# Two layers of windowed attention and a SiLU feed-forward net: chunk 2 of the first layer also by seven block products for eight

## The chip, the cores and the metric

The kernel runs on one core of a Trainium2 chip. The core has five engines with instruction streams of their own: TensorE (PE, matrix products into PSUM), VectorE (DVE), ScalarE (ACT), GpSimd (POOL) and SyncE (SP). In this kernel POOL and SP mostly issue DMA transfers. Measured is the time of one execution on the device in microseconds (us); lower is better.

## The reference

```python
x = A_x                                             # 1 x 2048 x 576, float32
x = x + _A_ref(_layernorm(x), A_wqkv, A_wo)
x = x + _B_ref(_layernorm(x), B_w1, B_w2)
x = x + _A_ref(_layernorm(x), A_wqkv, A_wo)         # the same weights again
x = x + _B_ref(_layernorm(x), B_w1, B_w2)

def _A_ref(x, wqkv, wo):                            # 32 heads of 18
    q, k, v = split(x @ wqkv)
    idx = pos[:, None] - (arange(8) * 2)[None, :]   # keys at 0, 2, .. 14 positions back
    logits = where(idx >= 0, einsum("bhsd,bhswd->bhsw", q, k[idx]) * 18 ** -0.5, -1e9)
    return einsum("bhsw,bhswd->bhsd", softmax(logits), v[idx]) @ wo

def _B_ref(x, w1, w2):                              # 576 -> 4608 -> 576
    return silu(x @ w1) @ w2
```

## The kernel before, in words

**Precision.** Each float32 operand of a product is split into two float16 parts (high and low), and three of the four partial products are made. A first FFN product over the 576 inputs thus takes 14 matmuls per 128 hidden units (the short last block of 64 inputs is packed), each over 512 tokens: 36 x 14 = 504 a chunk. The second FFN product takes three matmuls per pair of blocks.

**Tiling.** The 2048 tokens are four chunks of 512, so the two layers make eight steps, s = 0 to 7; "chunk 2" below is step 2, the third chunk of the first layer. Each step has a `front` (layer norm, q/k/v, attention in four units of eight heads, projection onto x, and the normalized and transposed input of the FFN), then an FFN. Attention itself runs on DVE: products with the window's keys (L756), sums over a head (L760), a softmax, products with the values (L789), sums over the window (L796, L797). For the first layer q, k and v of all chunks are made in step 0 (`qkv_ahead`) and wait in DRAM (`kd`, `qd`).

**Two FFN forms.** `ffn` is the plain one: a first product z (L1167), SiLU and high part on ACT, low part on DVE (L1174), and the second product in four groups into two accumulators `acc` (L1186), which DVE adds to x (L835). In step 0 it also loads the raw weights, scales and splits them (`raw_load`, `raw_split`), and stores the split forms to DRAM (`w1s`, `w2s`). `ffn_pairs` handles two blocks of 128 hidden units, two halves of the inputs and two halves of the tokens as a 2 x 2 block product, and makes seven block products (`P1` to `P7`) for eight, of 7 matmuls of 256 columns each: 18 x 7 x 7 = 882 a chunk (L1071). Their sums are put together on ACT (L1075) and DVE (L1078), the low part of h is L1104, and the second product is L1125. It needs seven linear forms of the inputs (`forms`, into tiles `xf`) and seven of the weights of each pair. `prepare` makes those of pair q, for q = 0 to 17: it loads raw blocks of w1 (POOL, L966 and L969), takes four sums on DVE (L977), splits them on ACT (L985) and DVE (L992), and stores seven blocks to `wfs[q]`. Before the change steps 0 to 2 use `ffn` and steps 3 to 7 use `ffn_pairs` (the constant S2).

**What sets the order.** The program is laid down by a planner (`Plan`). Each piece of work is given an engine, an assumed duration, what it reads and writes, buffers, and a priority (low first), and is taken when its inputs are there and a buffer is free; the result is one fixed order per engine. Step s has priority s - 1.0 for its front, s - 0.5 for its FFN's work on the other engines, and s + 0.5 for the FFN on PE. `prepare` has a priority of its own, PREP. Tiles of different names share memory as parts of one area (XA, XB, O, WQA, W1A, HSA, YO); the planner keeps two that overlap from being live at once.

## Time and profile before

| | |
|---|---|
| median of 3 runs | 2184.23 us (2181.3 to 2188.39) |
| profiled execution | 2180.11 us, span 2178.3 us |
| PE busy | 2125.9 us, 98% |
| DVE busy | 1585.8 us, 73% |
| ACT busy | 932.0 us, 43% |
| POOL busy | 379.4 us, 17% |
| granted PE clock, mean | 0.998 |

The sum of the prediction is made against the profiled execution, 2180.11 us, which lies 4.1 us under the median of the runs. A row of a group reads: source line, engine, operation, output <- inputs, shape, count, then busy time, mean duration of one in ns, and the idle time of the engine just before, with what ended it. The FFNs of the first layer begin and end on PE at about 227, 460, 699 and 932 us.

### The profile page before, as it was taken

The page shows a single profiled execution, that of the slowest core. Times are in us where ns is not written, and L with a number is a line of the kernel's source. Part 1 is how long each engine was busy: PE and PEld are TensorE (multiplying, and loading weights), DVE is VectorE, ACT ScalarE, POOL GpSimd, SP SyncE. Part 2 cuts the span into 40 slices and gives each one's busy share as a digit, 9 for nine tenths or more (in the row PEclk, how much of TensorE's full clock was granted, in tenths as well). Part 3 has the DMA queues.
Part 4 walks back from the last instruction along what each step waited for, and adds up shares of the span by engine and source line. Part 5 has one row for each costly group of instructions (what it writes and reads, how often), then busy time and mean ns, then how long its engine had stood idle before and what let it go on. Part 6 is the DMA issues. An engine that isn't in the chain of part 4 may idle for free.

```text
span 2178.3 us, 40221 instructions
## 1 busy us (share of the span) xinstructions
PE 2125.9 (98%) x15820; PEld 1540.8 (71%) x15820; DVE 1585.8 (73%) x2479; ACT 932.0 (43%) x1715; POOL 379.4 (17%) x639
## 2 busy tenths in 40 slices
PE   5999999999999999999999999999999999999999
PEld 3555556656766666677788778887688867888887
DVE  7898999999999754457975599646995569852222
ACT  7545677744244334343324434243442424333232
POOL 2124365332234331301100010000000000000000
PEclk9999999999999999999999999999999999999999
DMA  5577577586677675786649675496655855575443
GB/s 160 161 199 271 177 237 237 182 297 218 170 256 255 171 214 167 209 261 192 191 108 246 169 209 174 112 260 158 202 170 141 240 160 149 161 185 174 142 149 108
DMA packets 314006, 416.07 MB, mean 191 GB/s; under 512 B 136904, under 2 KB 237876, under 8 KB 307544
## 3 DMA queue, kind: packets, MB, share of 16 engines
q1 hardware_dynamic: 274832, 279.13, 45.2%
q0 software_dynamic: 35712, 129.17, 18.3%
q10 hardware_dynamic: 3272, 5.19, 0.8%
q8 instruction: 124, 2.03, 0.4%
q14 instruction: 66, 0.54, 0.1%
HBM read 298.47 MB, written 67.68 MB: 168 GB/s over the span
## 4 chain that ended last, share of the span: by engine, by line
PE 71%; DVE 15%; DMA 7%; issue 3%; POOL 1%; ACT 1%; ACTq 0%; SPq 0%; DVEq 0%; POOLq 0%
PE acc L1125 23%; PE z L1071 10%; PE misc L1071 10%; PE acc L1186 7%; PE z L1167 6%; PE z L658 6%; PE misc L658 5%; PE acc L828 4%; DVE pr L789 2%; DVE lg L760 2%; DMA w<-wfs 2%; DVE pr L796 2%; DVE pr L756 2%; DMA wq<-in_B_w_dram 1%; DVE xa L992 1%
## 5 line engine op out<-in xcount | busy, mean ns | idle before, releaser
L1125 PE MATMUL acc<-w,h 128*128 128x288 f16 x4320 | 544.9, 286 | 1.5 <-DVE h L1104 0.7
L1125 PEld LDWEIGHTS <-h 128*128 128x128 f16 x4320 | 422.5, 98 | 108.6 <-DVE h L1104 1.0
L1071 PEld LDWEIGHTS <-w 128*128 128x128 f16 x4410 | 430.8, 98 | 64.4 <-DMA w<-wfs 7.4
L1167 PE MATMUL z<-xb,w 128*128 128x512 f16 x1512 | 331.8, 379 | 6.4 <-ACT w L902 2.0
L1186 PE MATMUL acc<-w,h 128*128 128x288 f16 x2592 | 321.9, 286 | 0.0
L1186 PEld LDWEIGHTS <-h 128*128 128x128 f16 x2592 | 253.7, 98 | 65.7
L1071 PE MATMUL z<-xb,w 128*128 128x256 f16 x2240 | 281.9, 273 | 2.5 <-DMA w<-wfs 1.3
L1071 PE MATMUL misc<-xb,w 128*128 128x256 f16 x2170 | 273.4, 273 | 5.5 <-DMA w<-wfs 4.5
L1167 PEld LDWEIGHTS <-w 128*128 128x128 f16 x1512 | 147.5, 98 | 182.3 <-DVE w L904 3.7
L835 DVE SCALAR_TENSOR_TENSOR x<-acc,d,x 128x576 f32<-128x576 f32 x135 | 109.5, 812 | 192.3 <-PE acc L1125 151.5
L658 PEld LDWEIGHTS <-xa 128*128 128x128 f16 x1344 | 132.3, 99 | 119.6 <-issue 10.1
L756 DVE TENSOR_TENSOR pr<-qt,kv 128x2304 f32<-128x2304 f32 x64 | 163.5, 2554 | 33.6 <-DMA kv<-kv 32.2
L789 DVE TENSOR_TENSOR pr<-kv,pe 128x1152 f32<-128x1152 f32 x128 | 169.7, 1352 | 1.1
L760 DVE TENSOR_REDUCE lg<-pr 128x128 f32<-128x2304 f32 x64 | 163.1, 2548 | 1.2
L796 DVE TENSOR_TENSOR pr<-pr 128x1152 f32<-128x1152 f32 (+1 forms) x128 | 135.2, 1056 | 3.4
L1169 ACT ACTIVATE hs<-z,d 128x512 f32<-128x512 f32 x108 | 73.8, 683 | 123.1 <-PE z L1167 121.4
L1104 DVE SCALAR_TENSOR_TENSOR h<-wq,sh,h 128x1024 f16<-128x1024 f32 x59 | 75.5, 1280 | 60.9 <-ACT h L1101 60.9
L658 PE MATMUL z<-wq,xa 128*128 128x432 f16 x602 | 116.3, 349 | 3.4 <-ACT w L671 3.1
L828 PE MATMUL acc<-wo,yo 128*128 128x288 f16 x896 | 115.7, 288 | 3.3 <-DMA yo<-yh 3.3
L658 PE MATMUL misc<-wq,xa 128*128 128x432 f16 x574 | 111.8, 351 | 4.0 <-ACT xa L448 2.5
L1174 DVE SCALAR_TENSOR_TENSOR h<-hs,sh,h 128x512 f16<-128x512 f32 x108 | 79.6, 746 | 45.6 <-ACT h L1171 45.5
L1075 ACT ACTIVATE wq<-misc 128x256 f32<-128x256 f32 x85 | 32.0, 376 | 187.0 <-PE misc L1071 187.0
(196 smaller groups left out, 2355.1 us busy)
## 6 DMA issues: line engine op xcount, KB each, us to landing
w<-wfs SPq DMA_DIRECT2D x630, 160.0 KB, 3.3
w<-w2s SPq DMA_DIRECT2D x252, 288.0 KB, 4.8
w<-w1s SPq DMA_DIRECT2D x72, 320.0 KB, 4.8
wfs<-xa POOLq DMA_DIRECT2D x18, 1120.0 KB, 5.7
wq<-wqs SPq DMA_DIRECT2D x17, 1080.0 KB, 7.0
kv<-kd POOLq DMA_DIRECT2D x8, 1584.0 KB, 8.2
w1s<-w POOLq DMA_DIRECT2D x36, 320.0 KB, 3.8
w<-in_B_w_dram POOLq DMA_DIRECT2D x36, 288.0 KB, 4.6
```

Of the source, the lines that this page charges most:

```text
L658: nc.tensor.matmul(T(m)[:, :3 * UC], a, b, start=n == 0, stop=n == len(pl) - 1)
L756: nc.vector.tensor_tensor(T(pr), T(qt)[:, j:j + 2, None, :].to_broadcast([P, 2, W, UC]), win(T(kv), j, 2), op=ALU.mult)
L760: nc.vector.tensor_reduce(T(lg)[:, j:j + 2].rearrange("p a w h -> p (a w h)"), T(pr).rearrange("p a w (h d) -> p (a w h) d", d=DH), axis=A ...
L789: nc.vector.tensor_tensor(T(pr)[:, a].rearrange("p w (h d) -> p w h d", d=DH), v, T(pe)[:, j + a, :, :, None].to_broadcast([P, W, UH, DH]) ...
L796: nc.vector.tensor_tensor(t[:, :, 0:h, :], t[:, :, 0:h, :], t[:, :, h:2 * h, :], op=ALU.add)
L828: nc.tensor.matmul(T(acc)[:, h, 0:288], a, b[:, h * 288:(h + 1) * 288], start=n == 0, stop=n == len(pl) - 1)
L835: nc.vector.scalar_tensor_tensor(t, T(acc)[:, :, 0:288], d, t, op0=ALU.mult, op1=ALU.add)
L1071: nc.tensor.matmul(t, w[:, u, :], v[:, r, :], start=first and m == 0, stop=m == 6, skip_group_check=True)
L1125: nc.tensor.matmul(T(acc)[:, h, 0:288], T(hb[t])[:, a, f, j * P:(j + 1) * P], T(wbs[t][f])[:, w, h * 288:(h + 1) * 288], start=t == 0 and ...
L1167: nc.tensor.matmul(T(z), v, u, start=m == 0, stop=m == len(pl) - 1)
L1174: op("DVE", 0.68, lambda hs=hs, h=h, f=f: nc.vector.scalar_tensor_tensor(T(h)[:, 1, :], T(hs), shs[i][:, f:f + 1], T(h)[:, 0, :], op0=ALU. ...
L1186: nc.tensor.matmul(T(acc)[:, h, 0:288], T(hb[q])[:, a, j * P:(j + 1) * P], T(wbs[q][0])[:, w, h * 288:(h + 1) * 288], start=q == 0 and m = ...
```

## The change

Step 2 takes `ffn_pairs` as well (S2 goes from 3 to 2), so its front ends in `forms`, and `prepare` must be through the pairs before that FFN needs them: PREP goes from 1.6 to 0.9, ahead of step 2's attention. What comes with it:

- `forms` of step 2 keeps its second half of sums in a part of the key/value buffers (`yc`), since XA holds the weight forms being made; step 3's attention fetches its second and later units, and writes its output, only after these forms are done. Its first adds take a set of scratch buffers of their own (`ha`).
- `prepare` loads with eight DMAs instead of twelve, and stores its seven blocks as four and three, each from a tile of its own (`wg`, `wh`).
- In step 0 the raw w2 blocks from block 6 on land in XA (`wu`), and the split w1 blocks from 6 on in WQA (`wv`), once the last of the q/k/v products made ahead is done. Until now both shared the slots of `w1` and `w2`.

```diff
-PREP = 1.6
-S2 = 3
+FAR = 6
+PREP = 0.9
+S2 = 2
...
-    part("wg", XA, 1, [7, 5, P], F16)
+    part("wg", XA, 1, [4, 5, P], F16)
+    part("wh", XA, 1, [3, 5, P], F16, at=4 * KB * 2)
...
+    part("kv", KV, 2, [NI, 2, UC], F32)
+    part("yc", KV, 1, [8, KH], F32, at=KVB, turns=False)
...
+    part("wv", WQA, 6, [10, P], F16)
+    part("wu", XA, 4, [2, D], F16)
...
+    parts("ha", [(HSA, 0), (XB, 14 * KB * 2), (YO, 0)], [4, 2 * P], F32)
...
-                   own + [(qt, j) for j in range(NJ)] + [(kv, "halo"), (kv, "edge")], pr_, nbytes=P * 4 * UC * 26, lanes=2)
+                   own + [(qt, j) for j in range(NJ)] + [(kv, "halo"), (kv, "edge")], pr_, nbytes=P * 4 * UC * 26, lanes=2,
+                   after=formed[-1:] if u else ())
...
-                op("DVE", 2.55, tree, [], [(pr, 0), (pr, 1), (o, j, u), (o, j + 1, u)], pr_)
+                op("DVE", 2.55, tree, [], [(pr, 0), (pr, 1), (o, j, u), (o, j + 1, u)], pr_, after=formed[-1:])
...
-        a, b = raws[f] = Buf("w1"), Buf("w2")
+        far = f >= FAR
+        a, b = raws[f] = Buf("w1"), Buf("wu" if far else "w2")
...
-        wab = [(Buf("w1"), Buf("w2")) for f in fs]
+        far = f0 >= FAR
+        wab = [(Buf("wv" if far else "w1"), Buf("w2")) for f in fs]
...
-            for i in range(4):
-                f, h = divmod(i, 2)
-                c = slice((2 * q + f) * P, (2 * q + f + 1) * P)
-                nc.gpsimd.dma_start(t[:, i, 0:2, :], w1[h * KH:h * KH + 2 * P, c].rearrange("(k p) c -> p k c", p=P))
-            for r in range(4):
-                for h in range(2):
-                    nc.gpsimd.dma_start(t[32 * r:32 * (r + 1), h:4:2, 2, :], w1[
-                        h * KH + 2 * P:(h + 1) * KH, 2 * q * P:(2 * q + 2) * P].rearrange("p (f c) -> p f c", f=2))
-        op("POOL", 7.2, load, ["wsc"], [w], prio, nbytes=P * 12 * P * 4, lanes=8)
+            for h in range(2):
+                for k in range(2):
+                    nc.gpsimd.dma_start(t[:, h:4:2, k, :], w1[h * KH + k * P:h * KH + (k + 1) * P, 2 * q * P:(2 * q + 2) * P].rearrange(
+                        "p (f c) -> p f c", f=2))
+                for f in range(2):
+                    v = w1[h * KH + 2 * P:(h + 1) * KH, (2 * q + f) * P:(2 * q + f + 1) * P]
+                    nc.gpsimd.dma_start(t[:, h + 2 * f, 2, :], bass.AP(tensor=v.tensor, offset=v.offset, ap=[[0, 4], *v.ap]))
+        op("POOL", 4.8, load, ["wsc"], [w], prio, nbytes=P * 12 * P * 4, lanes=8)
...
-                hq, h = Buf("hq"), Buf("hp")
+                hq, h = Buf("hq" if s >= NC - 1 else "ha"), Buf("hp")
...
-        XT[s] = layer_norm(X[s], s - 1.0, "xb", s == 1, s == 0) if s < S2 else forms(X[s], s - 1.0)
+        XT[s] = layer_norm(X[s], s - 1.0, "xb", s == 1, s == 0) if s < S2 else forms(X[s], s - 1.0, "yc" if s == S2 else "yb", [("wfs", NP - 1, 1)] if s == S2 + 1 else [])
```

How the planner's order moves is seen at three places. Lines of the new file lie some 9 to 15 higher: L756 and L760 (attention) are L768 and L772 there, L835 is L847, L977 and L992 (preparation) are L991 and L1006, L1071, L1078, L1104 and L1125 (pairs) are L1086, L1093, L1119 and L1140, L1167, L1174 and L1186 (plain FFN) are L1182, L1189 and L1201, L828 (projection) is L840.

DVE at the end of chunk 0's FFN, from its last add to x (tile x_77) on; first before the change. `pr`, `lg`, `pe` and `o` are attention's tiles, `wq` and `xa` here the weights' sums and their splits.

```order
L835 SCALAR_TENSOR_TENSOR x_77<-acc_105,d_269,x_77 128x576
L789 TENSOR_TENSOR pr_89<-kv_83,pe_88 128x1152 x2
L796 TENSOR_TENSOR pr_89<-pr_89 128x2x576
L796 TENSOR_TENSOR pr_89<-pr_89 128x2x288
L797 TENSOR_TENSOR o<-pr_89 128x2x144
L1174 SCALAR_TENSOR_TENSOR h<-hs,sh_267,h 128x512
L756 TENSOR_TENSOR pr_89<-qt_84,kv_82 128x2304
```

After the change the same add is followed by this.

```order
L847 SCALAR_TENSOR_TENSOR x_77<-acc_105,d_268,x_77 128x576
L1006 SCALAR_TENSOR_TENSOR xa<-wq,accw,xa 128x4x256
L1006 SCALAR_TENSOR_TENSOR xa<-wq,accw,xa 128x4x128
L772 TENSOR_REDUCE lg_85<-pr_88 128x128
L1189 SCALAR_TENSOR_TENSOR h<-hs,sh_266,h 128x512
L1006 SCALAR_TENSOR_TENSOR xa<-wq,accw,xa 128x3x256
L1006 SCALAR_TENSOR_TENSOR xa<-wq,accw,xa 128x3x128
```

The preparation now stands among chunk 2's attention from here on, which moves later by as much.

DVE at the end of chunk 1's FFN, from its last add to x (tile x_81) on, before the change: the last of four units of chunk 3's attention among the plain FFN's work (`h`).

```order
L835 SCALAR_TENSOR_TENSOR x_81<-acc_106,d_270,x_81 128x576
L760 TENSOR_REDUCE lg_86<-pr_89 128x128
L769 TENSOR_REDUCE mx_90<-lg_86 128x32
L770 TENSOR_TENSOR lg_86<-lg_86,mx_90 128x256
L1174 SCALAR_TENSOR_TENSOR h<-hs,sh_267,h 128x512
L774 TENSOR_REDUCE mx_91<-pe_88 128x32
L775 RECIPROCAL mx_91<-mx_91 128x32
L776 TENSOR_TENSOR pe_88<-pe_88,mx_91 128x256
L789 TENSOR_TENSOR pr_89<-kv_83,pe_88 128x1152
```

After the change chunk 3's attention is in its second unit, and the adds of the pairs (L1093, from a bank of PSUM) stand between its long instructions.

```order
L847 SCALAR_TENSOR_TENSOR x_81<-acc_105,d_269,x_81 128x576
L772 TENSOR_REDUCE lg_85<-pr_88 128x128
L1093 TENSOR_TENSOR hs<-misc_102,hs 128x256
L1093 TENSOR_TENSOR hs<-z_100,hs 128x256
L1093 TENSOR_TENSOR hs<-z_101,hs 128x256
L768 TENSOR_TENSOR pr_88<-qt_84,kvs 128x2304
L772 TENSOR_REDUCE lg_85<-pr_88 128x128
L1093 TENSOR_TENSOR yo<-z_100,yo 128x256
L1093 TENSOR_TENSOR yo<-misc_103,yo 128x256
L1119 SCALAR_TENSOR_TENSOR h<-hs,sh_267,h 128x1024
```

A product of the pairs that needs such a bank again now stands behind an attention instruction of DVE.

PE at the start of chunk 2's FFN, before the change.

```order
L1186 MATMUL acc_106<-w_94,h 128x288
L1186 LDWEIGHTS h
L1186 MATMUL acc_106<-w_94,h 128x288
L1167 LDWEIGHTS w_70
L1167 MATMUL z_101<-xb,w_70 128x512
L1167 LDWEIGHTS w_70
```

After the change.

```order
L1201 MATMUL acc_105<-w_93,h 128x288
L1201 LDWEIGHTS h
L1201 MATMUL acc_105<-w_93,h 128x288
L1086 LDWEIGHTS w_70
L1086 MATMUL z_100<-xb,w_70 128x256
L1086 LDWEIGHTS w_70
```

The same place in the order now has products of half the columns, from the weight forms and the input's forms.

More of the change, by code (lines that the diff above doesn't have):

```diff
@@ L858, in raw_load @@
         late = marks[PACE_W[f]:PACE_W[f] + 1] if f < len(PACE_W) else ()
+        lb = [turned[-1]] if far else late
         def load_a():
@@ L1007, in sliding_attention_silu_ffn, with forms @@
     P_ORDER = ("P5", "P1", "P3", "P6", "P2", "P7", "P4")
-    def forms(xs, prio):
+    def forms(xs, prio, home="yb", late=[]):
         st, mv, nt = Buf("st"), Buf("mv"), Buf("nt")
@@ L1049, in forms @@
             out[n] = x
+        formed.append(done)
         return out
```

54 lines of the change are left out of this document (29 added, 25 removed).

## The prediction

> **What bounds the kernel now.** I read the page's parts 1, 2 and 4 first, then the engines by stage, then what TensorE (PE) waited for, then the groups of instructions.
>
> ```profile
> PE 2125.9 (98%) x15820; PEld 1540.8 (71%) x15820; DVE 1585.8 (73%) x2479; ACT 932.0 (43%) x1715; POOL 379.4 (17%) x639
> ...
> DVE  7898999999999754457975599646995569852222
> ...
> PE 71%; DVE 15%; DMA 7%; issue 3%; POOL 1%; ACT 1%; ACTq 0%; SPq 0%; DVEq 0%; POOLq 0%
> ```
>
> PE is busy for 98% of the span and carries 71% of the chain that ended last. VectorE (DVE) is the second: nine tenths or more in slices 4 to 13, half of that afterwards. The stages, cut where the first-layer FFNs begin and end (227 and 460 us for chunk 0, then chunk 1 to 699, chunk 2 to 932), show both. The columns are length, then busy time with count for PE, PEld, DVE, ACT, POOL, then granted clock, DMA share and GB/s.
>
> ```profile
> 227.00:460.00 233.00, 227.28 (x1490) 144.17 (x1490) 222.32 (x351) 164.15 (x282) 115.39 (x201) 1.00 0.69 227
> 460.00:699.00 239.00, 239.00 (x1569) 153.31 (x1568) 233.53 (x287) 91.40 (x121) 72.35 (x122) 1.00 0.70 223
> 699.00:932.00 233.00, 229.67 (x1480) 145.10 (x1479) 134.75 (x235) 88.17 (x139) 73.93 (x124) 0.99 0.69 199
> 932.00:1211.00 279.00, 277.50 (x2267) 221.11 (x2265) 199.19 (x324) 110.98 (x222) 21.24 (x34) 1.00 0.70 202
> ```
>
> Up to 699 us PE and DVE are both full (239.0 and 233.5 of 239.0), and PE still lost nothing there: DVE at 98% is no stall as long as its order suits. In chunk 2's FFN DVE has 98 us free. So PE's work is the time, and the question is what the moved DVE work costs PE. What PE waited for, from 460 to 1100 us (total, times, longest):
>
> ```profile
> PE acc L828 <- DMA yo<-yh: 3.3, 1, 3.3
> PE acc L1125 <- DVE h L1104: 0.7, 1, 0.7
> PE misc L658 <- DVE wq L1078: 0.6, 1, 0.6
> PE acc L1125 <- ACT h L1101: 0.2, 1, 0.2
> ```
>
> **Part 1: fewer products (removes PE work).** Chunk 2 loses 36 x 14 = 504 products of 512 columns (L1167) and gains 18 x 7 x 7 = 882 of 256 (L1071's form). The page's groups mislead here: neighbours overlap in the array, and L1071's two kinds of bank are counted apart. The second products (L1125 and L1186) are alike in both forms, 864 a chunk at 286 ns.
>
> ```profile
> L1125 PE MATMUL acc<-w,h 128*128 128x288 f16 x4320 | 544.9, 286 | 1.5 <-DVE h L1104 0.7
> ...
> L1186 PE MATMUL acc<-w,h 128*128 128x288 f16 x2592 | 321.9, 286 | 0.0
> L1071 PE MATMUL z<-xb,w 128*128 128x256 f16 x2240 | 281.9, 273 | 2.5 <-DMA w<-wfs 1.3
> L1071 PE MATMUL misc<-xb,w 128*128 128x256 f16 x2170 | 273.4, 273 | 5.5 <-DMA w<-wfs 4.5
> ```
>
> The busy time of one source line in a window (length, then PE with count, PEld with count) is free of that: L1071 over the whole span, five chunks; L1167 over the whole span, three chunks; L1167 in chunk 2's window.
>
> ```profile
> 0.00:2179.00 2179.00, 496.26 (x4410) 430.79 (x4410) 1.00 0.65 191
> ...
> 0.00:2179.00 2179.00, 331.83 (x1512) 147.48 (x1512) 1.00 0.65 191
> ...
> 699.00:932.00 233.00, 109.50 (x504) 49.17 (x503) 0.99 0.69 199
> ```
>
> A pair chunk is 496.26 / 5 = 99.3 us, a plain one 331.83 / 3 = 110.6: a gain of 11.4. Column counts alone (258,048 to 225,792, an eighth) would give an eighth of 110.6, 13.8: the far end. Chunk 2's own 109.5 against 99.3 gives 10.2: the near end. I take -11.4.
>
> The Trainium skill has a rule that speaks against the column count: "TensorE: Matmul & The Clock Gate", section "Wait — 56ns, not 53.3ns?", gives a warm matmul N / 2.4 GHz plus a fixed 2.5 ns or so, so that halving the columns pays the fixed part more often; an estimate by it is 504 x 215.8 - 882 x 109.2 = 12.5 us, and the sum below would be 1.1 lower. The rows stand 1.1 below it, their own waits included, and decide.
>
> **Part 2: the stall at the fourth chunk's projection (removes a wait).** The one large wait of this stretch is PE on the transposed attention output at 737 us; the rows of the timeline (start, length) around it:
>
> ```profile
> 740.77 4.93 PE L828 MATMUL acc<-wo,yo 128*128 128x288 f16 x28 [3.33 <-DMA yo<-yh]
> ...
> 759.01 3.59 PE L828 MATMUL acc<-wo,yo 128*128 128x288 f16 x28
> ```
>
> The 28 products after the wait took 4.93 us, the same 28 later 3.59: with the wait of 3.33 it cost 4.7. In the changed order this projection stands late in chunk 2's FFN, and DVE's rows ahead of it are worked off well before: summing the rows along both orders, PE's work ahead of the first of these products exceeds DVE's by 31 us against 13 in the kernel before. So the wait goes: -4.7 (ends: -4.7, and 0 if the transposes are late again behind SP's loads). Chunk 2's own projection moves too, by 45 us of PE work, and stands at 18 where it stood at 12 without a wait: 0.
>
> **Part 3: the preparation moves ahead (moves DVE, ACT, POOL and DMA work).** One pair's weights cost DVE four sums (L977) and four splits (L992), ACT four splits (L985), POOL's queue 12 loads (L966, L969) and one store, now 8 loads and two stores:
>
> ```profile
> L992 DVE SCALAR_TENSOR_TENSOR xa<-wq,accw,xa 128x1024 f16<-128x1024 f32 (+1 forms) x72 | 61.8, 911 | 0.7 <-ACT xa L985 0.6
> L985 ACT ACTIVATE xa<-wq,accw 128x1024 f16<-128x1024 f32 (+1 forms) x72 | 56.3, 842 | 108.2 <-DMA wfs<-xa 53.2 <-DVE wq L977 28.1 <-DMA wq<-in_B_w_dram 22.8
> L966 POOL DMA_DIRECT2D wq<-in_B_w_dram x72 | 51.0, 714 | 103.5 <-DVE xa L992 83.6 <-issue 16.8 <-DMA kv<-kd 1.6
> ...
> L977 DVE TENSOR_TENSOR wq<-wq 128x384 f32<-128x384 f32 x72 | 36.9, 553 | 1.0 <-issue 0.2
> ```
>
> On DVE that is (36.9 + 61.8) / 18 = 5.5 us a pair. By the end of chunk 1's FFN 8 pairs were done, now 13 are; one and a half of these already in chunk 0's, so that this stage gets +19 us, and 3 for chunk 2's forms in place of a plain normalization. Against it, 50 us of chunk 3's attention leave the stage for the next, and 10 of chunk 2's come in from the one before. Summed along the two orders with the means of all rows, less overlap, DVE has 211 us in this stage where it had 226, PE 226 in both: no loss, 0 (ends: -1, +3). ACT had 91 of 239 us there and gets 56.3 / 18 = 3.1 a pair more; POOL had 72, and has three transfers fewer a pair to issue. In chunk 2's stage DVE has 174 us where it had 131, PE 217: it fits as a whole.
>
> It doesn't fit in that stage's first half. From the first add of a pair (L1078) to the end of the second group's adds the new order has these on DVE: five of L756, six of L760, ten of L789, ten of L796, five of L797, fifteen small ones of the softmax (about 0.48 each), 33 of L1078, ten of L1104, eight of L835, and five pairs' preparation.
>
> ```profile
> L789 DVE TENSOR_TENSOR pr<-kv,pe 128x1152 f32<-128x1152 f32 x128 | 169.7, 1352 | 1.1
> L756 DVE TENSOR_TENSOR pr<-qt,kv 128x2304 f32<-128x2304 f32 x64 | 163.5, 2554 | 33.6 <-DMA kv<-kv 32.2
> L760 DVE TENSOR_REDUCE lg<-pr 128x128 f32<-128x2304 f32 x64 | 163.1, 2548 | 1.2
> L796 DVE TENSOR_TENSOR pr<-pr 128x1152 f32<-128x1152 f32 (+1 forms) x128 | 135.2, 1056 | 3.4
> L835 DVE SCALAR_TENSOR_TENSOR x<-acc,d,x 128x576 f32<-128x576 f32 x135 | 109.5, 812 | 192.3 <-PE acc L1125 151.5 <-PE acc L1186 40.8
> L1104 DVE SCALAR_TENSOR_TENSOR h<-wq,sh,h 128x1024 f16<-128x1024 f32 x59 | 75.5, 1280 | 60.9 <-ACT h L1101 60.9
> L1078 DVE TENSOR_TENSOR wq<-z,wq 128x256 f32<-128x256 f32 x92 | 37.7, 419 | 21.5 <-ACT wq L1075 12.8 <-PE z L1071 8.6
> L797 DVE TENSOR_TENSOR o<-pr 128x288 f32<-128x288 f32 x64 | 29.3, 458 | 2.6
> ```
>
> With the means of busy time over count: 28.1 + 13.3 + 10.6 + 2.3 + 7.3 + 13.5 + 12.8 + 6.5 + 27.4 = 121.8 us. PE has 476 pair products and 431 second products in the same piece, 476 x 0.1125 (496.26 / 4410) + 431 x 0.1261 (544.9 / 4320) = 107.9. DVE is 14 us over, and PE must wait for it (for a bank that an add frees, or for h), less what two accumulators and four banks let it run ahead. Both sums are a little high, since neighbours' records overlap, DVE's more. The ends are 0 (what 460 to 699 us shows: 98% full, no wait) and 14, and 5 more where an add also waits for ACT, as L1104 did in the row above. I take +6, nearer to the stretch that was as full and lost nothing.
>
> **Part 4: buffers of their own for chunk 0's later splits.** PE's largest wait in chunk 0's FFN was on the splits of pieces 4 and 5, which keep their buffers and their place in DVE's order, so it stays:
>
> ```profile
> PE z L1167 <- ACT w L902: 2.0, 1, 2.0
> PE z L1167 <- ACT hs L1169: 1.7, 2, 1.0
> ```
>
> The shorter waits behind it may shrink: 0, ends -2 and +2.
>
> **Sum.** -11.4 - 4.7 + 6 = -10.1 on the profiled execution's 2180.1 us: 2170.0. The median of the three runs shown, 2184.2, lies 4.1 above that execution, so 2174.1 is what I compare with it, 0.46% less. About 0.3%, 6.5 us, is what a measurement of this kernel can tell from no change: faster means below 2177.7, slower above 2190.8.
>
> **Rivals.** (a) The new DVE waits take the gain: PE waits the full 14 us, or the projection's wait of 4.7 stays. For it: DVE is full and in order, an add behind an attention multiply of 2.6 us holds PE. Against: chunk 4's attention already runs dense inside a pair FFN (199.2 us DVE busy, 932 to 1211 us), and PE lost 1.5 of 279. Time: -11.4 + 14 - 4.7 gives 2182, -11.4 + 6 gives 2179.
>
> (b) Slower: the loads of the preparation come late in the dense stretch and the sums (L977) hold DVE. The landing times of the same loads (KB, median us), 460 to 700 and then 700 to 930 us, and minimum, median and maximum of the first:
>
> ```profile
> wq<-in_B_w_dram POOLq DMA_DIRECT2D x32, 128.0 KB, 5.4
> ...
> wq<-in_B_w_dram POOLq DMA_DIRECT2D x36, 128.0 KB, 6.4
> ...
> DMA to landing us min/median/max: 2.8/5.4/11.2
> ```
>
> If each of 12 preparations came at the maximum instead of the median, DVE would stand 12 x 5.8 = 70 us. It has 226 - 211 = 15 to spare in the stage, and chunk 2's forms end 21 us of DVE work ahead of the stage's end, so chunk 2's FFN would start 70 - 36 = 34 us late: 2208. It decides from (36 + 10 + 6.5) / 12 = 4.4 us a preparation on. Against: no row shows DVE waiting for these loads (1.0 us before L977 in all). The Trainium skill, "SBUF — State Buffer", section "SBUF: two separate sides", warns that DMAs issued from GpSimd stand still while VectorE holds the port pair they share. By that rule the loads would be slower where DVE is fuller; the rows show the reverse, 5.4 against 6.4, so it gets little.
>
> (c) No new waits: PE reorders around all of them, and only parts 1 and 2 count: 2168.
>
> **How the numbers follow.** My forecast (2166 to 2177.7) has 0.5, (c) and still lower 0.12, (a) 0.26, (b) 0.12. Faster: 0.62; same 0.26; slower 0.12. The range 2164 to 2188 reaches from -11.4 - 4.7 - 4 over to (a) with 5 us more; it leaves out most of (b).
>
> **What would show it.** Right: 5292 products on L1086 (L1071 before) and some 595 us on it (6 x 99.3), 1008 on L1182; chunk 2's FFN about 11 us of PE work shorter; no wait above 1 us on the projection (L840); new PE waits on the adds (L1093) or on h in that FFN's first half, none above 2.5 us, 6 us in all; DVE at nine tenths up to some 800 us. Wrong: waits of PE there of 12 us or more, clock below 1.00 in that stage, DVE standing before L991, or chunk 1's projection waiting.

## The result, and the profile after

The changed kernel is slower by 0.42%: 2192.97 us median of 22 runs (2184.72 to 2201.41) against 2184.08 us of 22 runs of the kernel before (2178.84 to 2190.68), a ratio of 1.0042 with a 95% interval of 1.0031 to 1.0053. The forecast was 2174.1, so about 19 us are to be found. The profiled execution has a span of 2191.4 us; the one before had 2178.3 (2180.1 as a time), 4 us under the median of its runs.

The page's engine totals, its rows of DVE and of the granted clock, and the chain that ended last:

```profile
PE 2123.0 (97%) x16198; PEld 1579.9 (72%) x16198; DVE 1607.1 (73%) x2539; ACT 954.8 (44%) x1795; POOL 364.0 (17%) x585
...
DVE  7899999999987796548974589645995568852222
...
PEclk9999999999999899999999999999999999999999
...
PE 65%; DVE 7%; DMA 5%; issue 1%; POOL 1%; ACT 1%; SPq 0%; DVEq 0%; ACTq 0%
```

PE is busy for only 2.9 us less than before, where 11.4 us of products were to go, and idle for 2191.4 - 2123.0 = 68.4 us where it was idle for 52.4. The chain doesn't tell where the loss is: PE's share fell from 71% to 65% and DMA's from 7% to 5%, and the shares printed come to some 80% only. By stage, cut where the first-layer FFNs begin and end in this execution (columns as in the prediction):

```profile
223.30:462.00 238.70, 234.79 (x1548) 150.10 (x1548) 226.13 (x359) 168.53 (x289) 121.59 (x209) 0.99 0.72 235
462.00:700.60 238.60, 235.24 (x1511) 148.58 (x1510) 214.69 (x306) 105.88 (x160) 83.88 (x125) 0.99 0.84 235
700.60:937.10 236.50, 221.11 (x1860) 183.32 (x1858) 172.47 (x268) 98.20 (x183) 41.22 (x60) 0.96 0.79 228
```

Chunk 2's FFN, the stage that was to become some 11 us shorter, takes 236.5 us where it took 233. PE stands for 15.4 us of it, and the clock is 0.96. DVE's 214.7 and 172.5 us are near the 211 and 174 of the prediction. What PE waited for in that stage, and where on the timeline (start, length, and in brackets the wait ahead):

```profile
PE misc L1086 <- DMA w<-wfs: 10.7, 1, 10.7
PE acc L1140 <- DVE h L1119: 2.4, 1, 2.4
PE z L1086 <- DVE hs L1093: 1.6, 2, 1.4
PE misc L1086 <- DVE yo L1093: 0.5, 1, 0.5
PE misc L1086 <- DVE hs L1093: 0.3, 1, 0.3
```

```profile
727.74 1.68 PE L1086 MATMUL misc<-xb,w 128*128 128x256 f16 x7 [10.69 <-DMA w<-wfs]
729.93 1.65 PE L1086 MATMUL misc<-xb,w 128*128 128x256 f16 x7 [0.52 <-DVE yo L1093]
...
735.68 0.93 PE L1086 MATMUL misc<-xb,w 128*128 128x256 f16 x7
```

The waits on DVE come to 4.8 us. The large one is for a block of weight forms (`wfs`, loaded on SyncE's queue), 17 us into the stage. After it the same seven products take 1.68 us instead of 0.93: the clock is halved. The windows before, in and after the wait show it (the granted clock is third from the right, then DMA share and GB/s):

```profile
700.00:717.00 17.00, 14.65 (x115) 11.62 (x112) 13.61 (x15) 8.56 (x14) 5.21 (x8) 0.90 0.92 335
717.00:727.70 10.70, 0.05 (x1) 0.00 (x0) 0.00 (x0) 0.00 (x0) 6.86 (x10) 0.64 0.96 261
727.70:732.80 5.10, 4.55 (x21) 3.04 (x22) 3.31 (x4) 0.98 (x2) 0.00 (x0) 0.50 0.87 248
732.80:740.00 7.20, 7.20 (x63) 6.13 (x62) 6.71 (x9) 4.19 (x9) 0.00 (x0) 0.94 0.65 181
```

Why the block was late is read from SyncE's queue. There are slots for twelve blocks, and they were filled by 679 us; the thirteenth has to wait until the first products, from 700.6 on, free one. SyncE issued it at 713.8:

```profile
682.28 3.30 SPq L1061 DMA_TRANSPOSE xb<-yh  x2
685.68 1.34 SPq L1244 DMA_DIRECT2D x<-in_A_x_dram  x1
694.89 4.00 SPq L857 DMA_DIRECT2D w<-w2s  x6
705.04 0.33 SPq L1244 DMA_DIRECT2D x<-in_A_x_dram  x1
708.93 2.95 SPq L857 DMA_DIRECT2D w<-w2s  x2
713.83 16.05 SPq L1016 DMA_DIRECT2D w<-wfs  x11
```

The first row is the last two of the fourteen transposes of chunk 2's forms. From 698.9 to 713.8 SyncE mostly stands in front of transfers. Behind the last transpose, issued at 683.6, it had sent one load of x and six w2 blocks, eight transfers in all, and the ninth went out only when that transpose had landed; each one after it waited for the next oldest. The rows of the waits of SyncE's queue name them:

```profile
SPq L1244 <- DMA xb<-yh: 6.1, 1, 6.1
SPq L857 <- DMA x<-in_A_x_dram: 3.5, 1, 3.5
...
SPq L857 <- DMA w<-w2s: 2.2, 1, 2.2
```

The load of x at 705.0 waited for the transposes, which were issued by 685.6. The late issue is not all of the wait: blocks issued from 713.8 on were used from 727.7 on, and meanwhile x and w2 blocks ahead of them on that queue were still passing (58 to 75 packets of 2,304 bytes a us from 715 to 721). What else was under way are the fetches of chunk 3's keys (L712), which the change holds back until the forms are done, so that two go out right behind the transposes, at 683.7 and 690.8 us, on GpSimd's queue. Their duration:

```profile
L712 POOL DMA_DIRECT2D kvs<-kd x2: 536/537/538, 683.7 to 690.8; - x2
...
DMA to landing us min/median/max: 11.3/15.5/19.6
```

The packet records of the same execution, counted in stretches of 2 us, show both queues crawling (share of the 16 engines' time, then packets by their main sizes; 256 bytes are transposes, 12,672 key fetches). A packet is counted with its whole time in the stretch in which it starts:

```
        GpSimd's queue                        SyncE's queue
684      57%  5120 B x86                       41%  256 B x640
690     103%  12672 B x64                       4%  256 B x64
694     115%  4608 B x89, 12672 B x8          130%  256 B x374, 2304 B x18
696      27%  12672 B x11                       1%  256 B x19
702      41%  12672 B x15, 4608 B x16          32%  256 B x16, 2304 B x16
706      79%  12672 B x36, 4608 B x25          24%  2304 B x80
```

One transpose's 640 packets pass in 2 us at 684; those of the last take until about 704. The 28% at 696 does not mean that the engines stood idle: 14 packets that start between 695.4 and 696.3 last 1.6 to 8.0 us each (of 2,304 bytes 3.0 to 3.9 us where the median is 0.09, of 12,672 bytes 1.6 to 8.0 where it is 0.47). Counted over their whole length, packets fill the engines from 684 to 714. What fell is the rate, in the last column here:

```profile
689.00:692.00 3.00, 3.00 (x26) 2.39 (x25) 2.93 (x4) 1.44 (x2) 1.61 (x3) 1.00 1.05 415
696.00:698.00 2.00, 2.00 (x18) 1.59 (x17) 2.00 (x3) 0.00 (x0) 1.02 (x2) 1.00 0.28 72
```

So this is not plain lack of bandwidth; what held those packets the records don't show.

The rest of the loss, by profile. A step ends here with PE's last second product of its FFN; idle is the sum of PE's waits over 0.2 us. One row of the kernel before has to be put in its place first:

```profile
461.79 3.19 PE L1167 MATMUL z<-xb,w 128*128 128x512 f16 x14
```

These are the first 14 products of chunk 1's FFN (3.0 us up to the next product), which stand ahead of chunk 0's last group before the change and behind it after. The table counts them to step 1 in both. (Chunk 0's last group thus ends at 465.7 in the changed kernel, 3.7 us behind the cut at 462 above.)

| us | step 0 | step 1 | step 2 | steps 3 to 7 |
|---|---|---|---|---|
| before | 470.8 | 228.3 (idle 0.0) | 233.3 (idle 3.3) | 1245.9 |
| after | 465.7 | 235.1 (idle 3.3) | 236.6 (idle 15.2) | 1254.1 |

Step 0 gains 5.1, step 1 loses 6.8, step 2 loses 3.3, the later steps 8.2. In step 1 chunk 2's own projection now waits for its transposed attention output, and 6.8 us at half clock follow, which cost another 3.4:

```profile
PE acc L840 <- DMA yo<-yh: 3.3, 2, 3.0
```

In the later steps PE's waits come to 13.2 us instead of 10.2, and two spells of half clock are new. Over all the kernels below these steps lasted between 1246 and 1256 us without a pattern by edit, so the 8.2 are in part the luck of the two profiled executions.

### The profile page after: what moved, and what is told of

Its sections match the earlier page's. It is cut to its first block, busy times and chain, and to the rows that moved or that the text cites. A ratio compares the mean times of both kernels' runs of the same rounds, so it can differ in the third digit from the quotient of the medians.

```text
span 2191.4 us, 41290 instructions
## 1 busy us (share of the span) xinstructions
PE 2123.0 (97%) x16198; PEld 1579.9 (72%) x16198; DVE 1607.1 (73%) x2539; ACT 954.8 (44%) x1795; POOL 364.0 (17%) x585
## 4 chain that ended last, share of the span: by engine, by line
PE 65%; DVE 7%; DMA 5%; issue 1%; POOL 1%; ACT 1%; SPq 0%; DVEq 0%; ACTq 0%
PE acc L1140 25%; PE misc L1086 11%; PE z L1086 11%; PE z L669 4%; PE misc L669 4%; PE acc L840 4%; PE z L1182 3%; DMA w<-wfs 3%; PE acc L1201 3%; DVE xa L1006 1%; DVE pr L808 1%; DMA w<-w2s 1%; DVE pr L801 1%; DVE pr L768 1%; DVE lg L772 1%
## 5 line engine op out<-in xcount | busy, mean ns | idle before, releaser
L1140 PE MATMUL acc<-w,h 128*128 128x288 f16 x5184 | 655.2, 287 | 3.0 <-DVE h L1119 2.4
L1140 PEld LDWEIGHTS <-h 128*128 128x128 f16 x5184 | 507.3, 98 | 132.0 <-DVE h L1119 2.7
L1086 PEld LDWEIGHTS <-w 128*128 128x128 f16 x5292 | 519.6, 98 | 98.7 <-DMA w<-wfs 21.4
L1086 PE MATMUL misc<-xb,w 128*128 128x256 f16 x2618 | 334.2, 275 | 19.9 <-DMA w<-wfs 17.3
L1086 PE MATMUL z<-xb,w 128*128 128x256 f16 x2674 | 340.5, 275 | 5.5 <-DMA w<-wfs 1.6
L847 DVE SCALAR_TENSOR_TENSOR x<-acc,d,x 128x576 f32<-128x576 f32 x135 | 109.5, 812 | 177.0 <-PE acc L1140 170.7
L1201 PE MATMUL acc<-w,h 128*128 128x288 f16 x1728 | 215.1, 286 | 0.2 <-DVE x L847 0.2
L1201 PEld LDWEIGHTS <-h 128*128 128x128 f16 x1728 | 168.9, 98 | 44.6 <-issue 0.3
L768 DVE TENSOR_TENSOR pr<-qt,kvs 128x2304 f32<-128x2304 f32 x64 | 163.4, 2553 | 36.0 <-DMA kvs<-kvs 34.7
L801 DVE TENSOR_TENSOR pr<-kvs,pe 128x1152 f32<-128x1152 f32 x128 | 169.5, 1352 | 1.1
L772 DVE TENSOR_REDUCE lg<-pr 128x128 f32<-128x2304 f32 x64 | 163.1, 2548 | 1.2
L1182 PE MATMUL z<-xb,w 128*128 128x512 f16 x588 | 130.4, 382 | 4.7 <-ACT w L917 2.3
L1119 DVE SCALAR_TENSOR_TENSOR h<-wq,sh,h 128x1024 f16<-128x1024 f32 x60 | 76.8, 1281 | 72.6 <-ACT h L1116 72.6
L840 PE MATMUL acc<-wo,yo 128*128 128x288 f16 x896 | 117.6, 291 | 3.3 <-DMA yo<-yh 3.3
L1182 PEld LDWEIGHTS <-w 128*128 128x128 f16 x588 | 57.5, 98 | 74.8 <-issue 3.9
L669 PE MATMUL misc<-wq,xa 128*128 128x432 f16 x546 | 106.0, 350 | 3.9 <-ACT xa L457 2.5
L840 PEld LDWEIGHTS <-yo 128*128 128x128 f16 x896 | 88.7, 99 | 29.2 <-DMA yo<-yh 4.1
L749 POOL DMA_DIRECT2D kvs<-kvs x64 | 33.8, 535 | 376.5 <-ACT qt L739 374.3
L1182 PE MATMUL z<-xb,wq 128*128 128x512 f16 x420 | 93.6, 379 | 0.7 <-ACT hs L1184 0.7
```

What stands on the lines that cost most here:

```text
L669: nc.tensor.matmul(T(m)[:, :3 * UC], a, b, start=n == 0, stop=n == len(pl) - 1)
L768: nc.vector.tensor_tensor(T(pr), T(qt)[:, j:j + 2, None, :].to_broadcast([P, 2, W, UC]), win(T(kv), j, 2), op=ALU.mult)
L772: nc.vector.tensor_reduce(T(lg)[:, j:j + 2].rearrange("p a w h -> p (a w h)"), T(pr).rearrange("p a w (h d) -> p (a w h) d", d=DH), axis=A ...
L801: nc.vector.tensor_tensor(T(pr)[:, a].rearrange("p w (h d) -> p w h d", d=DH), v, T(pe)[:, j + a, :, :, None].to_broadcast([P, W, UH, DH]) ...
L840: nc.tensor.matmul(T(acc)[:, h, 0:288], a, b[:, h * 288:(h + 1) * 288], start=n == 0, stop=n == len(pl) - 1)
L847: nc.vector.scalar_tensor_tensor(t, T(acc)[:, :, 0:288], d, t, op0=ALU.mult, op1=ALU.add)
```

## The experiments

The theories: A, transposes and key fetches hold each other up, and SyncE's loads stand behind the transposes; B, the order on SyncE's queue alone is to blame; C, VectorE is over-full, as the prediction had it. Unless said, the order of all other instructions is exactly that of the changed kernel. Ratios are to the kernel before, measured beside each run, with 95% intervals.

### Key fetch after the transposes: e1

```diff
-                    q = nc.sync if s == 1 else nc.gpsimd
+                    q = nc.sync if s == 1 else nc.gpsimd; s == 3 and u == 1 and nc.gpsimd.tensor_copy(pace, T(lastx[0])[0:1, 0, 2 * P - 1:2 * P])
                     q.dma_start(T(kv).rearrange("p a b c -> p (a b c)"),
```

`lastx[0]` is the tile of chunk 2's last transposed form.

> The changed kernel with one instruction more: GpSimd copies one element of the last transposed form of chunk 2 before it issues the second fetch of chunk 3's keys, so that no key fetch is under way beside these transposes. The order of every engine is otherwise that of the changed kernel (2193 us). Theory A (the forms' last transposes, packets of 256 bytes, and the key fetches, packets of 12,672 bytes on GpSimd's queue, hold each other up; SP's loads stand behind the transposes, and PE waits 10.7 us at 717 us for a block of weight forms and then runs at half clock): the last transpose lands within 5 us of its issue, the wait at 717 falls below 3 us, and the kernel takes 2179 to 2183. Theory B (SP's order alone is to blame: eight w2 loads and an x load stand ahead of the thirteenth block of weight forms): the wait stays at 8 us or more, 2190 to 2196. Theory C (VectorE is over-full in that stage, and what PE waits for is its adds): the keys come later, so VectorE is later still; 2193 to 2199.

2188.79 us, 1.0018 (1.0005 to 1.0032). The fetches now leave at 691.8 and 693.4 and land sooner:

```profile
DMA to landing us min/median/max: 7.3/9.6/12.0
```

PE's wait falls to 7.9 us, not below 3. The fetches are faster with no transposes beside them, but they leave 8 us later and then pass beside the w2 blocks that stand ahead of the weight forms: from 700 to 704 the packet records count 22 to 30 key rows a us and 28 to 31 rows of 2,304 bytes, nearly one for one, where up to 176 of the latter pass in a us with nothing on GpSimd's queue (e14, at 705). The thirteenth block is issued 6.4 us after the FFN's first product, where it was 13.3 us. C is against the fall. B had 8 us or more, which 7.9 hardly refutes; A has only half of what it claimed.

### Key fetches on SyncE's queue: e2

```diff
-                    q = nc.sync if s == 1 else nc.gpsimd
+                    q = nc.sync if s == 1 or s == 3 and u else nc.gpsimd
```

> The changed kernel with the second to fourth fetch of chunk 3's keys and queries issued from SyncE's queue, the same that carries the transposes and the weight loads, at the same place in the program; all other instructions in the same order. Theory A: within one queue the fetches come after the transposes and cannot alternate with them, so the transposes land in 5 us and the wait at 717 us falls below 4 us; 2179 to 2184. A weaker form of A (the DMA engines are simply full, whichever queue the bytes come from): the wait stays at 6 to 11 us, 2188 to 2193. Theory B: the fetches stand ahead of the weight loads in SP's order too, the wait is as long or longer, 2192 to 2200.

2182.94 us, 0.9999 (0.9985 to 1.0013): 10 us of the loss are gone, with the same bytes at the same place in the program. B had the wait as long or longer here, so the order on SyncE's queue alone is not the cause. The wait that is left:

```profile
PE misc L1086 <- DMA w<-wfs: 4.3, 1, 4.3
```

### The parts of the change by themselves: e3 and e4

Both take S2 back to 3, and e3 takes PREP back to 1.6.

```diff
-S2 = 2
+S2 = 3
...
-    forms(X[s], s - 1.0, "yc" if s == S2 else "yb", [("wfs", NP - 1, 1)] if s == S2 + 1 else [])
+    forms(X[s], s - 1.0, "yb")
```

> The changed kernel with S2 back at 3 and PREP back at 1.6: of the change only the separate buffers in chunk 0's FFN, the eight loads and two stores of a preparation, and the new places of the scratch buffers are left. Against the kernel before (2184): the prediction gave this part 0, with ends of -2 and +2: 2182 to 2186. If the buffers bring what chunk 0's FFN start showed in the changed kernel (it began 3.7 us earlier), 2179 to 2181. If their gain is given back by new waits in chunk 0's FFN, 2186 to 2190.

> As the run with the buffers alone, but with PREP at 0.9: the preparation stands ahead of chunk 2's attention, and chunk 2 keeps its plain FFN with 504 products. It has the changed kernel's load on VectorE, on GpSimd's queue and on the DMA engines up to chunk 1's FFN, without the forms. If the move costs by itself (transposes of chunk 2's attention output late, as the 3.0 us wait at 595 us of the changed kernel has it): 3 to 8 us above the run with the buffers alone. If the forms and the pair FFN at chunk 2 make all of the loss: within 2 us of it.

e3: 2180.99 us, 0.9994 (0.998 to 1.0008). e4: 2180.29 us, 0.999 (0.9976 to 1.0003). Neither differs from before by more than is measured. So moving the preparation costs nothing that the time shows, though the projection of chunk 2 waits 4.6 us in e4's profile as well (an execution of 2188.9 us, the slowest of its twelve). The whole loss, 2193 against 2180, appears with S2 = 2: the forms, the held-back fetches, and the pair FFN.

### What is left after e2: e5, e6, e7

e5 sends the third unit's keys in four pieces between the weight blocks; e6 lets GpSimd wait for the 24th block before the next preparation's loads; e7 does both.

```diff
+                    if s == 3 and u == 2:       # e5, e7
+                        for n, (a, b) in enumerate(((0, 3), (3, 6), (6, 9), (9, NI))):
+                            late_.setdefault((14, 17, 20, 23)[n], []).append(lambda a=a, b=b: nc.sync.dma_start(
...
+            if 10 <= sent[0] < 24:              # e6, e7
+                late_.setdefault(24, []).append(lambda: (nc.gpsimd.tensor_copy(pace, sent[1][0:1, 0, 0:1]), load()))
+                return
```

> As the run with the fetches on SyncE's queue (2182.9 us, a wait of 4.35 us for weight forms in chunk 2's FFN), but the third of chunk 3's key fetches, whose data VectorE needs some 45 us after its issue, goes out in four pieces behind the 14th, 17th, 20th and 23rd block of weight forms of that FFN; the order of all other instructions is unchanged. Theory A (the blocks of weight forms are late because the key fetches take the DMA engines just then): the 4.35 us wait falls below 2 us and the half clock after it goes; 2176 to 2180. Theory D (what is left is the w2 loads ahead in SP's order and the preparation's loads on GpSimd's queue): the wait stays at 3 to 5 us; 2181 to 2185. If VectorE then waits for the pieces, its wait before the third unit's first product shows it.

> As the run with the fetches on SyncE's queue, but GpSimd holds the next two pairs' preparation loads (16 transfers, 1.6 MB) until the 24th block of weight forms of chunk 2's FFN has landed; they are needed some 25 us later. Theory A: the preparation's loads are a smaller part of the traffic, the wait of 4.35 us falls by 1 to 2 us; 2180 to 2183. Theory D: it falls below 2 us; 2176 to 2180. If the preparation becomes late, VectorE stands before the sums: above 2184.

> Both of the edits above together, beside the fetches on SyncE's queue. If traffic on the DMA engines is all that keeps the blocks of weight forms late, no wait of 2 us or more for them is left in chunk 2's FFN, the half clock there goes but for the one after VectorE's wait of 2.3 us, and the kernel takes 2174 to 2179, faster than before by 0.2 to 0.45%. If SP's order is the rest, a wait of 3 to 5 us stays and it takes 2181 to 2185.

In e6 and e7 one pair's weight forms are made from what its buffer held before its own blocks arrived. PE's waits in chunk 2's FFN, of e5 and then of e6:

```profile
PE z L1098 <- DMA w<-wfs: 3.1, 2, 2.8
PE acc L1152 <- DVE h L1131: 2.4, 1, 2.4
```

```profile
PE acc L1149 <- DVE h L1128: 5.0, 2, 2.6
PE z L1095 <- DVE hs L1102: 1.9, 2, 1.4
```

e5: 2182.16 us, 0.9995 (0.9981 to 1.0008). e6: 2183.63, 0.9999 (0.9984 to 1.0013). e7: 2185.68, 1.0011 (1.0 to 1.0022). e6 and e7 remove the wait for weight forms and DVE's take its place (5.0 and 6.6 us at L1140's line). None beats e2 by more than is measured, though step 2 shrinks from 230.0 to 226.1, 227.1 and 229.5 us; e7 has no wait for weight forms, as its first forecast had it, but not the 2174 to 2179 that went with it. What undoes the gain in the profiles of e5 and e7 is step 1: with one and the same order, chunk 2's projection waited 1.3 us (e6), 2.4 (e2), 2.9 (e1), 3.3 (after), 5.5 (e5) and 9.7 (e7).

### The fetches without the rest: e8

The kernel before, with two such transfers added ahead of chunk 3's pair FFN:

```diff
+                    if s == 2 and j < 2:
+                        nc.gpsimd.dma_start(dump[j], rows(kd[1][j], 0, [[NJ * 2 * UC, P], [1, NI * 2 * UC]]))
+                        nc.gpsimd.dma_start(dumq[j], rows(qd[1][j], 0, [[NJ * UC, P], [1, NJ * UC]]))
```

> The kernel before, with two transfers of the key fetch's size and rows (12,672 bytes each, and the queries' beside them) put on GpSimd's queue behind the first two stores of chunk 2's x, some 18 and 12 us ahead of chunk 3's pair FFN; they go from DRAM to DRAM and nothing waits for them. Nothing else changes. Theory A: PE then waits 4 to 11 us for weight forms some 10 to 17 us into chunk 3's FFN, where it waits 0 without them, and runs at half clock afterwards; 2189 to 2198 where the kernel before takes 2184. Theory B or C (order, or VectorE): no such wait, 2183 to 2186.

2187.55 us, 1.0015 (1.0004 to 1.0026). In chunk 3's FFN:

```profile
PE z L1073 <- DVE hs L1080: 2.8, 1, 2.8
PE acc L1127 <- DVE h L1106: 0.7, 1, 0.7
PE misc L1073 <- DMA w<-wfs: 0.6, 1, 0.6
```

PE waits 0.6 us for the blocks, not the 4 to 11 that A expected. So two large fetches ahead of the FFN do not by themselves make the blocks of weight forms that late. They are not free: VectorE stands 6.7 us for the next layer's x, a load on SyncE's queue beside the transfers, where it stands 0.5 in the kernel before, and its add for PE comes 2.8 us late. Nor is the test as close as e1: these transfers, from DRAM to DRAM, were through some 933 us, as the FFN began, while those of e1 ran 6 us into it. The next two runs take away one of the pair, fetch and transposes, where it stands.

### One of the pair left out: e9 and e10

```diff
-                   lambda f=f, a=a, x=x: nc.sync.dma_start_transpose(
+                   lambda f=f, a=a, x=x, n=n: (home, n) != ("yc", "P4") and nc.sync.dma_start_transpose(
```

```diff
                     row = blk * TB
+                    if s == 3 and u == 2: return
```

> The changed kernel without the last two of the 14 transposes of chunk 2's forms (the block product P4 then reads what stood in its tile before; nothing else is left out, and the order is the same). The key fetches go out at the same time from GpSimd's queue, but no transposes are under way beside them. Theory A (transposes and fetches hold each other up; the two fetches, 3.7 MB, then took 28 us, from 683.7 to 711.7, where the run with the gated fetches had them in 14): the fetches land by some 700 us, the wait at 717 falls from 10.7 us to below 4, and the kernel takes 2179 to 2186. Theory A' (the fetches' bytes alone keep the engines full, transposes or not): the wait stays at 7 us or more, 2188 to 2194.

> The changed kernel without the third key and query fetch of chunk 3 (that unit's attention reads the first unit's keys again); the order is the same. The second fetch still goes out at 683.7 us beside the last transposes. Theory A: the transposes are late by about half as much (landed by 692 to 696 instead of 704), and the wait at 717 falls to 2 to 6 us; 2181 to 2188. Theory A' (bytes): half the bytes are gone, the wait falls to 0 to 3 us; 2179 to 2184. Theory B (SP's order alone): 8 us or more, 2190 to 2196.

e9: 2184.47 us, 1.0001 (0.9981 to 1.002). e10: 2173.78, 0.9959 (0.9944 to 0.9974). The fetches of e9, issued at 681.8 and 688.9 from the same queue as in the changed kernel, and PE's wait for weight forms:

```profile
L712 POOL DMA_DIRECT2D kvs<-kd x2: 533/536/538, 681.8 to 688.9; - x2
...
DMA to landing us min/median/max: 9.4/10.0/10.6
```

```profile
PE z L1086 <- DMA w<-wfs: 1.0, 1, 1.0
```

Two transposes of 640 packets less, and the wait falls from 10.7 to 1.0 us (in an execution of 2175.0 us, the fastest of its ten). Step 2 lasts 224.4 us there, 12 less than in the changed kernel. In e10 no wait for a block is left, though the one remaining fetch still slows the last transposes (packets of 256 bytes trail until 704, 12 us after their issue). For e10 taken alone, the theory of bytes (A') had this wait right, and A had the transposes landed by 696; but A' had 7 us or more for e9, which has 1.0. Either partner taken away, the wait is gone or nearly so. e10 also shows what the change is worth without that wait and without one fetch: 10 us below before, and its step 2 takes 222.4 us.

### Order within one queue, and the projection's transposes: e11 to e14

e11 is e2 with chunk 2's attention output transposed on PE (`s < 3` for `s < 2` in `project`), which lets the planner lay out everything behind it anew. In e12 to e14 the fetches are planned for SyncE and wait in the plan for the last transpose; e13 and e14 put the third one behind the 28th block as well, and e14 transposes by DMA again. The lines shown are those of e13 and e14.

```diff
-                op("SP" if s == 1 else "POOL", 1.05, fetch, ...
-                   after=formed[-1:] if u else ())
+                op("SP" if s == 1 or s == 3 and u in (1, 2, 3) else "POOL", 1.05, fetch, ...
+                   after=(tr[-1:] + (wfo[27:28] if s == 3 and u == 2 else [])) if u else ())
```

> The run with the fetches on SyncE's queue, and besides chunk 2's attention output transposed on PE (36 small products and four copies on ScalarE) instead of by DMA, as chunks 0 and 1 have it. The wait of chunk 2's projection on those transposes came to 1.3 to 9.7 us in six profiles with the same order up to there. If early preparation's transfers beside these transposes cause it, it is gone: chunk 1's FFN lasts 227 to 229 us where it lasted 229 to 239, and the kernel takes 2177 to 2181. If PE's own transposes cost as much: 2182 to 2186.

> The changed kernel with the fetches of chunk 3's later units given to SyncE in the planner and placed behind the last transpose of chunk 2's forms, and chunk 2's attention output transposed on PE as in the run before. In that run a fetch stood between the last two pairs of transposes and PE waited 13.4 us; theory A (transposes and large fetches must not be under way together) says that the order alone decides: the wait falls to 2 to 5 us as in the first run with the fetches on SyncE's queue, and with the projection's wait gone the kernel takes 2177 to 2182. If placing them behind the transposes doesn't matter, the wait stays above 8 us, 2187 to 2192.

> As the run above, but the third unit's fetch is planned behind the 28th block of weight forms of chunk 2's FFN. With one fetch left out altogether the changed kernel took 2173.8 us, so a fetch that collides with nothing should bring it near: the wait for weight forms below 2 us, 2172 to 2178. If the fetch, coming later, makes VectorE late (its unit's first product some 40 us after the last transpose) or stands ahead of weight forms in SP's order: waits of 3 us or more, 2179 to 2185.

> As the run above, but chunk 2's attention output is transposed by DMA as in the changed kernel. It tells what PE's transposes are worth: with DMA the projection's wait (1.3 to 9.7 us so far) is back and it takes 2 to 5 us more than the run above if that wait is what makes chunk 1's FFN long; the same or less if PE's own 36 products and the copies cost as much.

e11: 2190.19 us, 1.0024 (1.001 to 1.0039). In its new order a fetch stands between the last two transposes on SyncE's queue, and the large wait is back:

```profile
725.04 1.68 PE L1086 MATMUL misc<-xb,w 128*128 128x256 f16 x7 [13.42 <-DMA w<-wfs]
```

e12, with the fetches behind the transposes, issues the thirteenth block 1.0 us after the first product (11.7 in e11), and its longest wait for a block is 3.8 us. But it takes 2192.07 us, 1.0028 (1.0015 to 1.0041), and e13 2193.23, 1.0037 (1.0024 to 1.005): the forecast times were missed, though e12's wait came as forecast. e13 and e14 differ by PE's transposes alone, and e14 takes 2178.13 us, 0.9976 (0.9963 to 0.9988). It is faster than the kernel before by 0.24%. Its engine totals, its waits in chunk 2's FFN, and that stage:

```profile
PE 2117.2 (97%) x16198; PEld 1578.6 (72%) x16198; DVE 1607.3 (74%) x2539; ACT 954.1 (44%) x1795; POOL 361.2 (17%) x579
```

```profile
PE misc L1087 <- DMA w<-wfs: 2.6, 3, 1.3
PE z L1087 <- DMA w<-wfs: 2.1, 1, 2.1
PE acc L1141 <- DVE h L1120: 0.7, 1, 0.7
```

```profile
697.00:926.50 229.50, 223.75 (x1914) 186.43 (x1912) 178.62 (x276) 97.73 (x184) 41.50 (x61) 1.00 0.81 241
```

No wait there is above 2.1 us, the clock stays at 1.00, and step 2 takes 223.9 us against 233.3 before. The projection's wait is larger than in the changed kernel (4.8 us), and the kernel is still the fastest of those that leave nothing out: that wait alone doesn't decide. PE's transposes remove it and lose 15 us elsewhere; in e13's profile step 2 has 14.4 us of waits, spread over blocks of weight forms (10.9) and DVE. Since the planner's order differs there, no run isolates the reason, and it stays open.

Delay of the thirteenth block behind the FFN's first product, and PE's longest wait for a block in that FFN, over the runs in which the first part of the order is alike:

| | after | e1 | e2 | e5 | e9 | e10 |
|---|---|---|---|---|---|---|
| thirteenth block, us | 13.3 | 6.4 | 6.7 | 3.2 | 3.3 | 2.0 |
| longest wait, us | 10.7 | 7.9 | 4.3 | 2.8 | 1.0 | none |

The delay is not all: e1 and e2 have it alike and wait 7.9 and 4.3 us. In e1 the keys pass beside the w2 blocks, in e2 they stand ahead of them on the same queue.

## Why the prediction was wrong

**Part 1, fewer products: right.** 5292 products stand on L1086 and 1008 on L1182. L1086 has 604.0 us, not 595, of which the half clock is a part. The gain is read in executions that have no half clock in step 2: with the plain FFN e4 takes 230.9 us there, 2.4 of them waits, so 228.5; with the pairs e10 takes 222.4 - 4.8 = 217.6 and e14 223.9 - 5.6 = 218.3, the latter with seven products of the next step (0.8). That is some 11 us, as forecast.

**Part 2, the stall at the fourth chunk's projection: half right.** Its 3.3 us wait is gone in the changed kernel (56 products at 863.8 without one). "Chunk 2's own projection moves too ... 0" failed: it waits 3.3 us there and PE then runs at half clock, 6.8 us of step 1 in all, and the wait is 1.3 to 9.7 us in six executions with the same order. Margins summed over DVE and PE say nothing of transposes that are slow. Why these differ so much from one execution to the next is open.

**Part 3, the preparation moves ahead: the step that failed.** Its DVE side held: the waits on adds and on h were forecast at 6 and came to 4.8, none above 2.4, and by e4 the move itself costs nothing that the time shows. But "it fits as a whole" was said of engines. The step counted the transfers of a preparation as time to issue them, and left out two things that the change's own lines had: fourteen transposes for chunk 2's forms, and the key fetches of chunk 3 that `after=formed[-1:]` releases in the same moment. Where they met, SyncE's queue came some 10 us late (the thirteenth block 13.3 us behind the FFN's first product, 3.3 in e9) and PE waited 10.7 us for it, with half clock behind. The forecast sum of -10.1 lacked this term altogether. e2 undoes it without touching any engine's work and takes back 10 us.

**Part 4, separate buffers: mis-sized by little.** Chunk 0's FFN, from its first product to its last and without the 14 of chunk 1, lasts 243.7 and 243.8 us with the old buffers (the kernel before and e8) and 240.5 to 242.3 in all kernels with the new ones. That is some 2 us, where I had 0 with ends at -2 and +2. The rest of step 0's 5.1 us lies ahead of this FFN, which begins between 223.3 and 227.0 us whatever the kernel. On the time of e3 not more than 2180.99 against 2183.83 is seen, which its interval doesn't tell from nothing.

**The rivals.** (a), DVE's waits, came as forecast and not as a rival. (b) had the right sign and the wrong load: the preparation's weights were not late, the forms' were. (c) is what e14 and e10 approach: 2178 and 2174 against the 2168 of (c).

**The sum by steps.** -5.1 + 6.8 + 3.3 + 8.2 is, but for rounding, the 13.1 us that separate the two profiled executions. The forecast -10.1 was meant for step 2, which got 3.3: 13.4 of the 23 us between forecast and outcome, and e9, with two transposes less, has 12 of them back. Step 1 adds 6.8, the wait that Part 2 put at 0. Of the later steps' 8.2 no run shows a cause.

## What to carry to other kernels

Where a change holds a transfer back until something is done, look up what else starts at that moment and on which queues, and count the transfers and not only the engines: here two 1.9 MB fetches met the last transposes, and the queue that carries the weights stood behind them. Put a large transfer behind the transposes on the same queue, neither beside them on another nor between them, and give it a later place if its data are needed later. e2 and e14 are faster than the changed kernel with it; e12 and e13 have that order too and are slower than the kernel before, for a reason that was not found. And count a wait of PE with the half clock that follows it.

## What the runs showed of the hardware

- A DMA transpose of 640 packets passed in some 2 us (at 684, 626 of them in the first us with 11 packets of GpSimd's queue beside them) and took about 20 us from its issue beside a fetch with 12,672-byte rows on another queue; the two fetches (keys and queries of a unit, 1.9 MB each) took 28 us from the first issue to the last landing, 683.7 to 711.7, against 17.6 in e9 without those transposes. The Trainium skill, "Advanced Engine Details and Errata", section "X-Bar Transpose (TRN2)", has transposes as fast as regular DMAs. The trace doesn't agree: 626 packets of 256 bytes in a us are 160 GB/s, where 415 GB/s passed from 689 to 692, and beside the fetch it was far less.
- Two queues with work take turns: from 689 to 692 the records count 27, 33 and 31 transpose packets a us and 31, 33 and 31 key rows. The Trainium skill, "DMA: Bandwidth & Descriptors", section "Queues, rings and completion order", says that each DMA engine takes turns between the queues packet by packet, and the trace agrees there. It doesn't explain the 20 us: a fetch has only eight such rows for each of 16 engines, under 40% of the transpose's packets had passed by 695, and 301 more passed in the next us. The last 100 took until 704, while packets of 2,304 and 12,672 bytes lasted up to 3.9 and 8.0 us; in e11 the fetch stood on the transposes' own queue, and the wait was 13.4 us. What holds such packets stays open.
- By the rows above SyncE had at most eight transfers under way, and one late transpose, the oldest, held all that stood behind it for 6.1 us.
- The granted clock falls to one half in spells of about 3.4, 6.8 and 13.7 us (from 713, 597 and 720 us on in the changed kernel's records). The changed kernel has six between 230 and 1830 us, behind waits of PE of 1.8 to 10.7 us. One of 2.4 us in the kernel before (at 1290) brought none. The Trainium skill, "TensorE: Matmul & The Clock Gate", section "Part 1: The HAM clock gate", has an activity window of some 3.4 us, and half clock after an idle one: the spells are multiples of it, but here waits shorter than the window were enough. The mean clock, 0.991 against 0.998, is some 30 us more at half clock, working and waiting, between the two profiled executions, a loss of at most 15 us.
